# Score products in 64-column pairs, a separate place for each engine's part of a step, and a new order, in a fused attention and MLP kernel

## The chip, the cores and the metric

One core of one Trainium2 chip runs the whole program. The metric is the device time of one execution in microseconds (us). Engines are named as in the profile: PE (matrix products; PEld is its weight loads), DVE, ACT and POOL (elementwise work), SP (which issues nearly all transfers).

## What is computed

A linear attention with a decaying state, for 4 batches x 8 heads, 768 steps, head size 40, and behind it a gated MLP with a spatial gate over the sequence:

```python
for t in range(S):                       # attention, per batch and head
    y[t] = r[t] @ state
    Sa = state @ a[t]
    state = state * w[t][None, :] - outer(Sa, b[t]) + outer(v[t], k[t])
x = y as (4, 768, 320)                   # the heads side by side
h = gelu(x @ w_in)                       # 1024 columns
u, v = h[:, :512], h[:, 512:]
v = layernorm(v) * g_ln
v = w_sg @ v + b_sg                      # 768 x 768, over the sequence
out = x + (u * v) @ w_out
```

## The kernel before, in words

**Attention.** The 768 steps are cut into 12 chunks of 64 (`C`). Within a chunk the recurrence becomes matrix products and the inverse of a unit triangular 64x64 matrix for each of the 32 (batch, head). A chunk goes through these stages:

- *Gates*, once per batch: `gate_w` (L259) to `gate_k` (L314). DVE scans the decays (`ex`, `hs`), DVE or POOL multiplies them into `at` and `kb`, PE forms the products `ab` and turned copies of `kb` (`gate_4`, L289), DVE masks `ab` into `at` (`gate_a`), ACT copies the block to be inverted into `nts` (`gate_n`) and the turned `kb` into `kbt` (`gate_k`).
- *Inverse*, once per chunk for all 32: DVE turns the 32x32 blocks (`inv_in`, L319, tile `n`). Then `steps` (L328) does elimination steps, each a product `tg` and a sum `x`; for the chunks 2 to 11 POOL does them all but the last one, which is DVE's with the tile `tv`. In chunk 0 DVE and POOL share them, in chunk 1 DVE does the first step. `inv_back` (L373), `inv_g` (L385) and `inv_x` (L397) turn the result back and join the four 32x32 blocks with PE products (`gp`, `xp`) and ACT copies into `xt`.
- *Chain*, once per batch: `chain1` (L426) forms `ru`, `chain_t` (L436) turns the state (`tp`), `chain2` (L444) applies the inverse, `chain3` (L455) forms the next state (`sp`, first the old state through a 128-column identity product, then 8 pairs of products for the heads) and turns `vu` (`ut`), `chain4` (L481) forms the scores (`pq`, four products with 128 weight columns and 128 columns of data) and masks them on DVE (`pqs`), `chain5` (L490) forms the outputs (`yp`), which DVE scales (`yt`) and SP writes to the DRAM buffer `xd`.

Products in fp32 run on PE in several passes: the profile counts two for one matmul of the code, so 8 for the four score products of a batch.

**MLP.** The class `Mlp` reads `xd` back (`load_x`) and splits it into a high and a low fp32r half (`split_x`: `xh`, `xl`). Its pieces are `v0` to `v5` (`in_v`, PE tile `hv`, 8 products of 512 columns), `u0` to `u7` (`in_u`, `hu`), `s0` to `s7` (`sgu`, `sg`, 18 products of 384 columns) and `o0` to `o5` (`outp`, `op`, 10 to 12 products of 384 columns). A `v` piece ends in a normalised and split pair `vh`, `vl`, an `s` piece in a gated and split pair `gy`, `gx` (DVE twice, ACT, POOL). The weights of the gate are split into `wsh` on ACT and `wsl` on POOL or DVE (`part_sg`, string `SGE`); the output weights come as 64-bit numbers and go through `split64` (L710: ACT, DVE twice, ACT, POOL three times; tiles `sc`, `stg`, `lt`, `woh`, `wol`).

**Order.** Every engine executes its instructions in program order (class `InOrder`), so order is written out by hand. A chunk has 28 positions, a half of a chunk 14. `half` (L510) gathers the steps with their positions and sorts them: `CH` places the twelve chain steps of each half (a step is placed as a whole, with its PE, ACT and DVE parts), `GPOS` the gates, `START`, `BACK` and `GX` the inverse, `DEC` and `DSTEP` the conversion of the input weights, `FILL` and `AFTER` five MLP pieces and their elementwise parts within the last chunk. The first chunk's prologue (L567 to L588) has positions of its own: `T0` to `T4`, `TB0`, `TB1`, `ZERO`, `SECOND`, `EX`, and a letter per batch that says whether DVE (`V`) or POOL (`G`) does a gate product (`E0A`, `E0K` for chunk 0, `E1A`, `E1K` for chunk 1). Behind the chunks `Mlp.run` (L980) goes through the list `SEQ0` for batch 0 (mixed with the `v` and `u` pieces of batch 1) and `SEQ` for the others; `SGS`, `OUTS` and `OSTEP` say before which piece the weight conversions stand, and `XL` how many pieces ahead x is loaded.

Of the kernel before, what the change touches and what calls it, by code (L numbers as in the profile page):

```python
# [17 lines left out]
C = 64  # L18
# [3 lines left out]
DF = 1024  # L22
# [14 lines left out]
T0 = 6.16  # L37
T1 = 16.87
T2 = 5.22
TB0 = 4.1  # L40
TB1 = 11.89
# [3 lines left out]
T3 = 10.0  # L45
T4 = 16.8
CH = ((1.45, 2, 4, 5.28, 4.96, 7.81, 8.16, 12.33, 4.53, 10.76, 13.17, 14.9), (-1.88, 1.21, 7.06, 5.51, 8.13, 7.67,
    10.0, 10.99, 3.41, 8, 12, 14.21))
GPOS = (((0.34, 0.33, 0.61, 1.31, 3.87, 4.25, 4.26, 4.27), (2.52, 2.51, 2.79, 3.49, 5.81, 6.43, 6.44, 6.45), (5.06,
# [4 lines left out]
GE = ("VVVVV", "VVV", "V", "V")  # L54
START = (13.13, 0.58)
E0A = "GGGG"
E0K = "GVGG"
E1A = "GGGG"
E1K = "GVGG"
BACK = (17.88, 23.11, 26.9, 23.92)  # L60
GX = (24.68, 4.6)
# [4 lines left out]
DSTEP = ((-12.34, -2.5, 0.0, 0.98, 2.18, 3.84), (-13.26, -0.81, 0.0, 0.49, 2.66, 3.52))  # L66
DEC = ((275.05, 0), (277.2, 0), (283.29, 0), (288.37, 0), (292.22, 1), (298.29, 1), (299.11, 1), (306.81, 0),
    (311.6, 1), (314.23, 1), (324.86, 1), (328.18, 1))
# [3 lines left out]
FILL = (("x0", 0, 321.35), ("v0", 0, 329.24), ("v1", 0, 345.97), ("v2", 0, 347.7), ("u0", 0, 349.9))  # L72
AFTER = {"v": (0.56, 0.57, 1.47, 1.61, 1.95, 2.3, 2.4, 4.11, 4.8), "u": (0.5, 1.09, 1.99, 2.04), "x": ()}
# [5 lines left out]
SEQ0 = (("x1", 0), ("x0", 0), ("v0", 0), ("u3", 0), ("u0", 0), ("u1", 0), ("v2", 0), ("u2", 0), ("v1", 0), ("v3",  # L79
# [14 lines left out]
IS = 1  # L94
ROWS = (12, 26)
EX = ((0.01, 0, 0.3, 0.6, 1.5, 2.6, 2.61, 2.62), (0.01, 0, 0.3, 0.6, 1.5, 2.6, 2.61, 2.62))
# [47 lines left out]
def attention(tc, a, xd, flag, keep, ps, mlp=None):  # L144
# [4 lines left out]
    with ExitStack() as ctx:  # L149
# [73 lines left out]
        for i, t in enumerate(nts):  # L223
            for h in range(2):
                (V, G, G)[i].memset(t[64 * h + 32:64 * h + 64, :, 32:64], 0.0)
# [30 lines left out]

        gate, unit, x1_of, st2, pqt = {}, {}, {}, {}, {}
# [10 lines left out]
        def gate_2(c, b, E=V):  # L268
# [5 lines left out]
            E.tensor_tensor(out=at[:, :, 1], in0=kab[:, 1], in1=ex[:, :, 0:C], op=ALU.mult)  # L274
            A.copy(out=at[64:128, :, 0], in_=at[0:64, :, 1])

# [12 lines left out]
        def gate_4(c, b):  # L289
            kb, at = gate.pop((c, b)), ats[ent(c, b)]  # L290
            ab = gate[c, b] = ps("ab0"), ps("ab1")
            for p in range(NP):
                for h in range(2):
                    r = slice(64 * h, 64 * h + 64)
                    for x in range(2):
                        T.matmul(ab[h][64 * x:64 * x + 64, C * p:C * p + C], lhsT=kb[r, p, x], rhs=at[r, p, 1],
                                 start=True, stop=True, tile_position=(64 * h, 64 * x), skip_group_check=True)
# [3 lines left out]
        def gate_a(c, b):  # L301
            ab, at = gate[c, b], ats[ent(c, b)]
            for h in range(2):
                V.tensor_tensor(out=at[0:64, :, h], in0=ab[h][0:64, 0:256].rearrange("p (q x) -> p q x", x=C),
                                in1=mask[0:64].unsqueeze(1).broadcast_to([64, NP, C]), op=ALU.mult)

        def gate_n(c, b):
            nt, q0 = nts[c % 3], 4 * b
            for h in range(2):
# [4 lines left out]
        def gate_k(c, b):  # L314
            for g in range(2):
                A.copy(out=kbts[ent(c, b)][:, 160 * g:160 * g + 160].rearrange("p (q h x) -> p q h x", q=2, h=2),
                       in_=gate[c, b][g][:, 256:512].rearrange("p (q h x) -> p q h x", q=2, h=2)[:, :, :, 0:D])

        def inv_in(c):  # L319

            n = iv.tile([128, 32, 32], F32, name="n", bufs=2)
# [62 lines left out]

        def inv_g(c):  # L385
            nt, gs, x1z = nts[c % 3], gss[0], x1_of[c]
            gp = ps("gp")
            for q in range(NQ):
                for h in range(2):
                    r = 64 * h  # L390
                    T.matmul(gp[r + 32:r + 64, 32 * q:32 * q + 32], lhsT=nt[r:r + 64, q, 32:64],
                             rhs=x1z[r:r + 64, q], start=True, stop=True, tile_position=(r, r + 32))
            gv = gp.rearrange("p (q x) -> p q x", x=32)
# [3 lines left out]
        def inv_x(c):  # L397
# [7 lines left out]
            xv = xp.rearrange("p (q x) -> p q x", x=32)  # L405
            A.copy(out=xt[0:32, :, 32:64], in_=xv[0:32])
            A.copy(out=xt[64:96, :, 32:64], in_=xv[64:96])

        rus = {}
# [15 lines left out]

# [703 lines left out]
```

## Time and profile before

| | us |
|---|---|
| median of 3 runs (650.85 to 651.57) | 651.53 |
| the profiled execution | 653.22 |
| its span in the trace | 650.8 |

| engine | busy us | share of the span | instructions |
|---|---|---|---|
| PE | 584.3 | 90% | 9038 |
| PEld | 527.0 | 81% | 9038 |
| DVE | 509.4 | 78% | 1079 |
| ACT | 393.7 | 60% | 1106 |
| POOL | 394.5 | 61% | 881 |

The rows of the trace count from the start of the span. A timeline row gives start, duration of the whole group, engine, line, operation, output tile, inputs, shapes and the number of instructions in the group; in brackets stands how long the engine had been idle before it, and what ended that. All instructions have the line L130, since a helper records them, so tiles are told by their names. The granted clock of PE is given as a share of its full rate; 0.50 is the lower of its two levels.

### The profile page before, as it was taken

What the parts mean: (1) busy time and instruction counts of PE and PEld (TensorE: products, weight loads), DVE (VectorE), ACT (ScalarE), POOL (GpSimd) and SP (SyncE); (2) the same over time, 40 slices, a digit from 0 to 9 for tenths busy, and PEclk for the clock granted to TensorE, in tenths of its full rate; (3) what the DMA queues carried; (4) which work ended last, traced back from release to release, by engine and by line L of the source; (5) the groups of instructions that cost most, each with busy time, mean ns of one, the idle gap of its engine ahead of it and who ended that gap; (6) DMA issues with size and microseconds to landing.
All of it is one profiled execution on the core that took longest, in us unless ns stands there. A gap on an engine that the chain in (4) does not pass through costs nothing.

```text
span 650.8 us, 22488 instructions
## 1 busy us (share of the span) xinstructions
PE 584.3 (90%) x9038; PEld 527.0 (81%) x9038; DVE 509.4 (78%) x1079; ACT 393.7 (60%) x1106; POOL 394.5 (61%) x881
## 2 busy tenths in 40 slices
PE   6435899999999999999897999696999999999996
PEld 5334788888888888888786888596989999999995
DVE  7898977979779788797586789877888768567732
ACT  5535888888988879798573756442345336324410
POOL 6367888888888888888887344566442433332321
PEclk8556899999999999999977799798999999999999
DMA  7731333444444443334433316310003003010001
GB/s 238 213 101 42 106 105 106 118 108 119 112 112 117 117 120 108 103 98 104 117 101 85 109 40 181 120 56 17 31 1 104 26 7 103 1 32 13 20 29 38
DMA packets 57618, 56.55 MB, mean 87 GB/s; under 512 B 35936, under 2 KB 47456, under 8 KB 57504
## 3 DMA queue, kind: packets, MB, share of 16 engines
q1 hardware_dynamic: 57504, 55.02, 29.5%
q8 instruction: 73, 1.20, 0.8%
q14 instruction: 41, 0.34, 0.2%
HBM read 47.14 MB, written 7.86 MB: 85 GB/s over the span
## 4 chain that ended last, share of the span: by engine, by line
PE 40%; DVE 21%; POOL 20%; issue 8%; ACT 7%; DMA 2%; SPq 0%; POOLq 0%; ACTq 0%; DVEq 0%
PE sg L130 11%; POOL x L130 9%; POOL tg L130 9%; PE op L130 5%; PE ab L130 4%; PE hu L130 4%; PE hv L130 3%; PE sp L130 3%; PE pq L130 2%; PE yp L130 2%; PE ru L130 2%; DVE sc L130 2%; DVE v L130 2%; DVE x L130 2%; DVE g L130 2%
## 5 line engine op out<-in xcount | busy, mean ns | idle before, releaser
L130 POOL TENSOR_TENSOR x<-x,tg 128x100 f32<-128x100 f32 (+8 forms) x348 | 131.8, 379 | 27.0
L130 POOL TENSOR_TENSOR tg<-x,n 128x100 f32<-128x100 f32 (+8 forms) x348 | 125.4, 360 | 29.3 <-DVE x L130 2.2
L130 POOL TENSOR_TENSOR gx<-g,gy 128x384 fp32r<-128x384 f32 x32 | 33.2, 1041 | 79.7 <-ACT gy L130 79.7
L130 PE MATMUL sg<-wsh,vh 128*128 128x384 f32 x192 | 67.1, 350 | 4.3 <-ACT vh L130 3.6
L130 PE MATMUL sg<-wsl,vh 128*128 128x384 f32 x192 | 66.6, 347 | 3.7 <-POOL wsl L130 3.0
L130 ACT ACTIVATE nts<-ab 32x256 f32<-32x256 f32 x192 | 62.2, 324 | 10.6 <-DVE at L130 7.8
L130 PE MATMUL sg<-wsh,vl 128*128 128x384 f32 x192 | 66.7, 347 | 0.8 <-POOL vl L130 0.8
L130 PE MATMUL ab<-at,kb 64*64 64x64 f32 x1536 | 42.2, 241 | 22.2 <-POOL kb L130 13.6
L130 ACT CAST gy<-g 128x384 fp32r<-128x384 f32 x32 | 16.5, 515 | 70.7 <-DVE g L130 66.9
L130 PEld LDWEIGHTS ab<-at,kb 64*64 64x64 f32 x1536 | 33.9, 148 | 30.9 <-POOL kb L130 15.6
L130 PE MATMUL pq<-rt,vut 128*128 128x128 f32 x384 | 56.3, 291 | 0.3 <-DVE yt L130 0.3
L130 PEld LDWEIGHTS pq<-rt,vut 128*128 128x128 f32 x384 | 48.2, 197 | 2.8 <-DVE yt L130 0.4
L130 PE MATMUL yp<-pqs,kbt 128*64 128x64 f32 x768 | 49.6, 235 | 0.0
L130 PE MATMUL yp<-rt,s 80*40 80x64 f32 x704 | 46.0, 231 | 0.0
L130 ACT CAST vh<-v 128x512 fp32r<-128x512 f32 x24 | 14.9, 622 | 50.2 <-DVE v L130 50.2
L130 POOL TENSOR_TENSOR rs<-rs,mhalf 128x1 f32<-128x1 f32 x24 | 13.5, 562 | 49.7 <-DVE rs L130 43.9
L130 POOL TENSOR_TENSOR vl<-v,vh 128x512 fp32r<-128x512 f32 x24 | 31.7, 1322 | 18.4 <-ACT vh L130 18.3
L130 PEld LDWEIGHTS yp<-pqs,kbt 128*64 128x64 f32 x768 | 40.1, 147 | 2.7 <-issue 1.1
L130 PEld LDWEIGHTS sg<-wsh,vh 128*128 128x128 f32 x192 | 37.4, 195 | 5.1 <-ACT vh L130 4.0
L130 PEld LDWEIGHTS sg<-wsl,vh 128*128 128x128 f32 x192 | 37.6, 196 | 4.6 <-POOL wsl L130 3.4
L130 DVE SCALAR_TENSOR_TENSOR g<-sg,gl,bt 128x384 f32<-128x384 f32 x32 | 19.7, 615 | 25.5 <-PE sg L130 24.4
L130 DVE TENSOR_TENSOR at<-ab,mask 64x256 f32<-64x256 f32 x96 | 35.8, 408 | 3.9 <-PE ab L130 3.2
(139 smaller groups left out, 1681.1 us busy)
## 6 DMA issues: line engine op xcount, KB each, us to landing
main<-main SPq DMA_DIRECT2D x88, 160.8 KB
vu<-vs SPq DMA_DIRECT2D x24, 160.0 KB
vs<-vb SPq DMA_DIRECT2D x24, 160.0 KB
rt<-rt SPq DMA_DIRECT2D x48, 80.0 KB
vut<-vt SPq DMA_DIRECT2D x24, 160.0 KB
xd<-yt SPq DMA_DIRECT2D x96, 40.0 KB
xt<-xd SPq DMA_DIRECT2D x16, 192.0 KB
out<-y SPq DMA_DIRECT2D x16, 192.0 KB
```

What stands on the lines that cost most here:

```text
L130: return self.tc.keep_in_program_order(f(*a, **k))
```

## The change

Scores: each of the four products of a batch becomes two with 64 weight columns, which write the two halves of the same output (`PQ`). State: the identity product is split into two of 64 columns and the head products load 40 weight columns instead of 64 (`MK`). `gate_4` runs its two inner loops in the other order. `gate_c`, the ACT copy of `gate_2`, gets a position of its own, and so does each engine's part of `inv_g`, `inv_x` and the chain steps (`LAG`, `GL`); a part whose position falls behind the end of a half goes into the next one (`tail`). Two gate products of the prologue go from POOL to DVE (`E0A`, `E1A`). In the last chunk six products that nothing reads, of 128 weight columns and 512 columns of data, stand at position 348.88 (`JUNK`). In the MLP the piece `v1` of batch 1 goes from before `s5` to behind `s4`, the last batch gets an order of its own (`SEQL`: `s6` and `s7` before `o0`), its last pairs `gy` and `gx` use tiles of `v` pairs that are free by then, and the weight conversions shift. All positions are set anew. `NS` is 0, so its branches aren't taken; they are left out below, as are assertions on the order.

```diff
-T0 = 6.16
-T1 = 16.87
-T2 = 5.22
+T0 = 7.03
+T1 = 16.19
+T2 = 3.25
...
-E0A = "GGGG"
+E0A = "VGGG"
-E1A = "GGGG"
+E1A = "GGVG"
...
-FILL = (("x0", 0, 321.35), ("v0", 0, 329.24), ("v1", 0, 345.97), ("v2", 0, 347.7), ("u0", 0, 349.9))
+FILL = (("x0", 0, 318.12), ("v0", 0, 332.67), ("v1", 0, 345.97), ("v2", 0, 345.98), ("u0", 0, 349.9))
...
-    0), ("s0", 0), ("s3", 0), ("v1", 1), ("v0", 1), ("s5", 0), ("s4", 0), ("o1", 0), ("u0", 1), ("o0", 0), ("v2",
-    1), ("o2", 0), ("s6", 0), ("s7", 0), ("v5", 1), ("u1", 1), ("v3", 1), ("v4", 1), ("u4", 1), ("o5", 0), ("o3",
+    0), ("s0", 0), ("s3", 0), ("v0", 1), ("s5", 0), ("s4", 0), ("v1", 1), ("o1", 0), ("u0", 1), ("o0", 0), ("v2",
+    1), ("o2", 0), ("s6", 0), ("s7", 0), ("u1", 1), ("v3", 1), ("v4", 1), ("v5", 1), ("u4", 1), ("o5", 0), ("o3",
...
-XL = 3
+XL = 2
-SGS = (2, 5, 5, 6, 8, 10, 10, 13, 12, 13, 14, 13)
-OUTS = (11, 12, 12, 14, 15, 16, 17, 18)
-OSTEP = (-2, 0, 0, 0, 0, 1)
-SGE = "GGGGGVGGGVGG"
+SGS = (2, 5, 3, 6, 8, 10, 10, 13, 14, 13, 14, 13)
+OUTS = (11, 12, 12, 14, 15, 18, 19, 18)
+OSTEP = (-2, 0, 0, 0, 0, 0)
+SGE = "GGGGGVGVGVGG"
...
-SECOND = (18.63, 0.02)
-ZERO = 3.22
+SECOND = (18.03, 0.07)
+ZERO = 3.51
...
+PQ = 1
+MK = 40
+JUNK = ((348.88, 6),)
...
+SEQL = ("s1", "s2", "s0", "s3", "s4", "s5", "s6", "s7", "o0", "o1", "o2", "o3", "o5", "o4")
...
         def gate_4(c, b):
...
-                for h in range(2):
-                    r = slice(64 * h, 64 * h + 64)
-                    for x in range(2):
+                for x in range(2):
+                    for h in range(2):
...
         def chain3(c, b):
...
-                    T.matmul(sp[:, 0:NP * D], lhsT=ident, rhs=sc.rearrange("p q x -> p (q x)"), start=True, stop=True,
+                for h in range(2 if IS else 0):
+                    r = slice(64 * h, 64 * h + 64)
+                    T.matmul(sp[r, 0:NP * D], lhsT=ident[:, r], rhs=sc.rearrange("p q x -> p (q x)"), start=True, stop=True,
                              skip_group_check=True)
                 for p in range(NP):
                     for h in range(2):
                         l0 = 2 * D * p + D * h
-                        T.matmul(sp[64 * h:64 * h + 64, D * p:D * p + D], lhsT=kbt[:, l0:l0 + 64],
+                        T.matmul(sp[64 * h:64 * h + m, D * p:D * p + D], lhsT=kbt[:, l0:l0 + m],
...
         def chain4(c, b):
...
-            for g in range(4):
-                T.matmul(pq[:, 128 * g:128 * g + 128], lhsT=vut[:, g], rhs=rt[:, :, g], start=True, stop=True)
+                for g in range(4):
+                    for x in range(2 if PQ else 0):
+                        T.matmul(pq[64 * x:64 * x + 64, 128 * g:128 * g + 128], lhsT=vut[:, g, x], rhs=rt[:, :, g], start=True,
+                                 stop=True, skip_group_check=True)
...
         def half(c, hf, side):
...
+            def put(k, fs):
+                d = lag[k] if len(fs) > 2 else (lag[k],)
+                for y, f in zip((0, *d), fs):
+                    add(z[k] + y, f)
...
+    def idle(self, n):
+        o = self.ps("idle")
+        for _ in range(n):
+            self.T.matmul(o, lhsT=self.wih[:, 0, HF:HF + 128], rhs=self.wih[:, 0, HF:DF], start=True, stop=True,
+                          skip_group_check=True)
```

## Rows read from the trace of the kernel before

**Rows 1.** Windows view: PE, PEld, DVE, ACT, POOL busy (instructions), clock, DMA share, GB/s.

```profile
75.00:351.00 276.00, 266.53 (x6403) 234.42 (x6402) 223.88 (x480) 225.58 (x691) 228.27 (x610) 0.98 0.40 110
```

**Rows 2.** Groups of POOL from 75 to 350 us: count, busy, mean ns, idle before.

```profile
L130 POOL TENSOR_TENSOR x<-x,tg 128x78 f32<-128x78 f32 (+4 forms) x303 | 116.6, 385 | 23.7
L130 POOL TENSOR_TENSOR tg<-x,n 128x78 f32<-128x78 f32 (+4 forms) x304 | 111.0, 365 | 23.8
```

**Rows 3.** Timeline of DVE and POOL in the prologue, and the last inversion step.

```profile
17.99 0.91 DVE L130 TENSOR_TENSOR at<-ab,mask 64x256 f32<-64x256 f32 x2 [1.38 <-PE ab L130]
31.15 1.28 DVE L130 TENSOR_TENSOR x<-x,tv 128x115 f32<-128x115 f32 x1
49.87 2.08 DVE L130 STREAM_TRANSPOSE n<-nts 128x1024 f32<-128x1024 f32 x1
...
52.44 0.24 POOL L130 TENSOR_TENSOR tg<-x,n 128x30 f32<-128x30 f32 x1 [2.22 <-DVE x L130]
...
350.81 0.25 POOL L130 TENSOR_TENSOR x<-x,tg 128x30 f32<-128x30 f32 x1
```

**Rows 4.** Groups by shape: one product of the gates on DVE.

```profile
L130 DVE TENSOR_TENSOR at<-main,ex 128x256 f32<-128x256 f32 x40 | 21.6, 540 | 0.0
```

**Rows 5.** Timeline of PE, narrow windows: scores, outputs, next chunk's sums, state.

```profile
255.50 0.61 PE L130 MATMUL pq<-rt,vut 128*128 128x128 f32 x4
...
255.83 0.28 PE L130 MATMUL pq<-rt,vut 128*128 128x128 f32 x1
256.04 0.29 PE L130 MATMUL ab<-at,kb 64*64 64x64 f32 x4
...
257.52 0.67 PE L130 MATMUL sp<-vu,kbt 128*64 128x40 f32 x16
...
260.25 0.28 PE L130 MATMUL yp<-rt,s 80*40 80x64 f32 x4
260.36 0.32 PE L130 MATMUL ru<-vs,at 128*64 128x40 f32 x6
```

**Rows 6.** Timeline: chunk 3's matrices turned on DVE, first used by POOL.

```profile
99.25 2.20 DVE L130 STREAM_TRANSPOSE n<-nts 128x1024 f32<-128x1024 f32 x1
...
105.75 0.24 POOL L130 TENSOR_TENSOR tg<-x,n 128x31 f32<-128x31 f32 x1
```

**Rows 7.** Timeline of PE: 18 products of the sixth `sgu` piece.

```profile
436.58 0.34 PE L130 MATMUL sg<-wsh,vh 128*128 128x384 f32 x1
...
438.67 0.34 PE L130 MATMUL sg<-wsh,vh 128*128 128x384 f32 x1
442.05 0.44 PE L130 MATMUL sg<-wsl,vh 128*128 128x384 f32 x1 [3.04 <-POOL wsl L130]
...
443.07 0.52 PE L130 MATMUL sg<-wsh,vh 128*128 128x384 f32 x1
...
446.27 0.41 PE L130 MATMUL sg<-wsl,vh 128*128 128x384 f32 x1
```

**Rows 8.** Timeline of POOL before that wait, of DVE after it.

```profile
440.19 0.80 POOL L130 TENSOR_TENSOR wol<-stg,lt 128x256 fp32r<-128x256 f32 x1
440.95 1.04 POOL L130 TENSOR_TENSOR wsl<-ws,wsh 128x384 fp32r<-128x384 f32 x1
...
449.98 0.60 DVE L130 SCALAR_TENSOR_TENSOR g<-sg,gl,bt 128x384 f32<-128x384 f32 x1
```

**Rows 9.** Waits of PE from 400 to 460 us: total, times, longest.

```profile
PE hv L130 <- DVE xh L130: 1.5, 1, 1.5
PE op L130 <- ACT gy L130: 1.2, 1, 1.2
PE op L130 <- POOL gx L130: 0.9, 2, 0.5
```

**Rows 10.** Waits of PE from 640 us to the end.

```profile
PE op L130 <- POOL gx L130: 0.5, 1, 0.5
PE op L130 <- ACT gy L130: 0.4, 1, 0.4
```

More of the change, by code (lines that the diff above doesn't have):

```diff
@@ L317, in gate_k @@
                        in_=gate[c, b][g][:, 256:512].rearrange("p (q h x) -> p q h x", q=2, h=2)[:, :, :, 0:D])
+            seen.add(("kt", c, b))
         def inv_in(c):
+            for h in range(2 if NS else 0):
+                r = slice(64 * h + 32, 64 * h + 64)
+                A.copy(out=nts[c % 3][r, :, 0:32], in_=nts[c % 3][r, :, 32:64])
             n = iv.tile([128, 32, 32], F32, name="n", bufs=2)
@@ L427, in chain1, with mm @@
             at, vs, rb = ats[ent(c, b)], vss[b // 2][:, b % 2], rhsb[b]
-            ru = rus[b] = ps("ru")
             k = 128 if c else 64
-            for p in range(NP):
-                for h in range(2):
-                    T.matmul(ru[64 * h:64 * h + 64, D * p:D * p + D], lhsT=at[0:k, p, h],
-                             rhs=vs[0:k, p, h], start=True, stop=True, skip_group_check=True)
-            A.copy(out=rb, in_=ru[:, 0:NP * D].rearrange("p (q x) -> p q x", x=D))
+            def mm():
+                assert not c or ("vs", c, b) in seen
+                assert ("at", c, b) in seen
+                ru = rus[b] = ps("ru")
+                for p in range(NP):
+                    for h in range(2):
+                        T.matmul(ru[64 * h:64 * h + 64, D * p:D * p + D], lhsT=at[0:k, p, h],
+                                 rhs=vs[0:k, p, h], start=True, stop=True, skip_group_check=True)
+                seen.add(("c1", c, b))
@@ L436, in chain_t, with out, mm @@
+            def out():
+                A.copy(out=rb, in_=rus[b][:, 0:NP * D].rearrange("p (q x) -> p q x", x=D))
+                seen.add(("rb", c, b))
+            return mm, out
         def chain_t(c, b):
-            if c:
-                tp = ps("tp")
+            def mm():
+                tp = tps[b] = ps("tp")
                 for g in range(2):
                     T.transpose(out=tp[0:80, 128 * g:128 * g + 128], in_=scs[b][:, 2 * g:2 * g + 2], identity=ident)
+                seen.add(("ct", c, b))
@@ new lines, in mm, with out @@
+            def mm():
+                assert ("rb", c, b) in seen and ("xt", c) in seen
+                ru = rus[b]
+                for p in range(NP):
+                    for h in range(2):
+                        r = slice(64 * h, 64 * h + 64)
+                        T.matmul(ru[r, 160 + D * p:160 + D * p + D], lhsT=xt[r, 4 * b + p], rhs=rb[r, p],
+                                 start=True, stop=True, tile_position=(64 * h, 64 * h), skip_group_check=True)
+            def out():
+                uv = rus[b][:, 160:320].rearrange("p (i g x) -> p i g x", i=2, g=2)
+                for h in range(2):
+                    A.mul(out=vu[64:128, :, h], in_=uv[64 * h:64 * h + 64], mul=-1.0)
+                seen.add(("vu", c, b))
@@ L472, in chain3, with copies @@
                 V.tensor_tensor(out=sc[0:e], in0=ts, in1=bc(cn[0:e], [e, NP, D]), op=ALU.mult)
+                seen.add(("sc", c, b))
+            def copies():
+                if c == NCH - 1:
+                    return
+                assert ("c1", c, b) in seen and ("sc", c, b) in seen
                 for h in range(2):
@@ L481, in chain4, with out @@
+            def out():
+                assert ("tn", c, b) in seen and (not c or ("c4", c - 1, b) in seen)
+                A.copy(out=vuts[b // 2][0:80, b % 2, :, 1], in_=uts[b][0:80, 0:256].rearrange("p (q t) -> p q t", q=4))
+                seen.add(("ut", c, b))
+            return mm, state, copies, turn, out
         def chain4(c, b):
             rt, vut = rts[b // 2][:, b % 2], vuts[b // 2][:, b % 2]
-            pq = ps("pq")
-            for g in range(4):
-                T.matmul(pq[:, 128 * g:128 * g + 128], lhsT=vut[:, g], rhs=rt[:, :, g], start=True, stop=True)
@@ new lines, in mm @@
+            def mm():
+                assert ("ut", c, b) in seen
+                pq = pqt[b] = ps("pq")
+                for g in range(4):
+                    for x in range(2 if PQ else 0):
+                        T.matmul(pq[64 * x:64 * x + 64, 128 * g:128 * g + 128], lhsT=vut[:, g, x], rhs=rt[:, :, g], start=True,
+                                 stop=True, skip_group_check=True)
+                    if not PQ:
+                        T.matmul(pq[:, 128 * g:128 * g + 128], lhsT=vut[:, g], rhs=rt[:, :, g], start=True, stop=True)
+                seen.add(("c4", c, b))
@@ L510, in half, with loads @@
+        def loads(f, stage, c, bs, *a):
+            assert all((stage, c, b) in seen for b in bs)
+            f(*a)
         def half(c, hf, side):
@@ L953, in side @@
                 at(PX1, lambda: self.load_x(1, 0))
+            for p, k in JUNK:
+                at(p, lambda k=k: self.idle(k))
             for x, b, p in FILL:
@@ L974, in piece @@
             self.sgu(b, k % 4, k // 4)
+        elif x[0] == "j":
+            self.idle(k)
         elif x[0] == "o":
```

219 lines of the change are left out of this document (140 added, 79 removed), and 9 rows, old and new, of the table GPOS.

## The prediction, made before the changed kernel was run

> **What bounds the kernel now.** I read the share of each engine by stretches first. From 75 to 351 us PE is busy for 266.5 of 276 us at a clock of 0.98, and POOL for 228 [rows 1]: two engines that look near their limit, so the groups of instructions have to say which one sets the pace. On POOL the elimination sums and products take 116.6 and 111.0 us, with 23.7 and 23.8 us of idle time before them, and no releaser is named for that idle time [rows 2]. Together that is 275.1 of 275 us: POOL goes from one step to the next, and the gaps of some 80 ns are its own. In this stretch POOL sets the pace, chunk after chunk, and PE is only almost as long. The third view is the timeline around it. POOL's first step of the long series starts at 52.44 and its last sum stands at 350.81 [rows 3], so the time has three parts: a prologue of 52.4 us, a POOL chain of 298.6 us (with the last sum's 0.25), and a tail of 299.7 us to the end of the span at 650.8.
>
> The prologue hangs on DVE, which runs from its first scan to the block that it turns at 49.87 with small holes only; POOL waited 2.22 us for it [rows 3]. The tail is read from the waits of PE, which has the most work there.
>
> The sum below is made against the profiled execution, 653.2 us, which lies 1.7 us above the median of 651.5; the last step takes 1.7 off.
>
> **The change part by part.**
>
> *Scores.* The last four of a batch's eight score passes start from 255.50 on, the very last at 255.83, and the next kind at 256.04 [rows 5]. So a pass takes 0.11 us, and the last one 0.21: some 0.10 is the price of going over to another shape of tile. The change makes 16 passes of 64 columns of weights. Output products in such a shape go four in 0.11 us (260.25 to 260.36), that is two at a time at the pace of one full pass, and from there to the sums of the next chunk no 0.10 is seen [rows 5]. Two halves side by side thus cost what one full product does, and spare up to two changes of shape, some 0.1 to 0.2 us a batch. Against this stands a rule. The Trainium skill, in "TensorE: Matmul & The Clock Gate", section "Part 3: Packing small matmuls", says that a weight load overlaps with running products only when it goes to another group of rows. Both halves use all 128 rows, so by that rule they would run in turn, and the scores would double. The pace of the outputs in rows 5, which have the same form, speaks against it; it is a rival below.
>
> *State.* Eight pairs take from 257.52 on 0.67 us of a group, loads of 64 columns [rows 5]. Loading 40 columns can at best save three eighths of what the load sets, some 0.1 to 0.2 us a batch, and at worst nothing; the identity in two halves is priced like the scores, at nothing. Scores and state together save some 0.3 us a batch, 1.2 a chunk, on PE.
>
> *What of it counts in the middle.* Nothing, as long as POOL goes on without a gap [rows 2]. PE's savings there only lengthen its lead. If POOL's cover were gone, ten chunks by 1.2 us plus the order would be worth about 16 us at most, but no edit here touches POOL's steps. The new positions can do harm only if an input of POOL comes late: the blocks of chunk 3 are turned from 99.25 to 101.45 and first used at 105.75 [rows 6], a lead of 4.3 us. I take 0, with a bound of nothing below and, for a late block, the rival below. The same holds for the separate places of ACT's and DVE's parts, the other loop order in `gate_4` and the ACT copy `gate_c`: ACT is busy for 226 and DVE for 224 of the 276 us [rows 1], and both end ahead of POOL.
>
> *Prologue.* Chunk 1's gates start two positions earlier, zeros are loaded later, and two products go from POOL to DVE. On DVE they add 2 x 0.54 = 1.1 us [rows 4]. In return DVE's hole of 1.38 us before the masking at 17.99 [rows 3], with a smaller one ahead of it 1.7 us in all, has a filling: the masking waited for PE, PE for POOL's products. And sums such as the one at 31.15 took 1.28 us; a smaller one of the kind took 0.25 on POOL at 350.81 [rows 3]. There are two of these, both while POOL works on gate products; with POOL relieved they should shrink by 1.0 each. That gives -1.7 + 1.1 - 2.0 = -2.6. Bounds: +1.1 if neither hole nor contention goes, -4 if smaller contended operations shrink too.
>
> *Last chunk.* Six score groups of a batch lie between 351 and 400 us, where PE has no POOL chain beside it: -1.2 with the state products. The six idle products are 512 columns; products of 384 go at 0.174 us (12 from 436.58 to 438.67 [rows 7]), so one is 0.232 by columns and six 1.4 us. They stand between other work, not in a wait that I can name, so I count +1.3 to +1.4; the lower bound is 0 if PE would have waited there. Together +0.1. PE's wait for `xh`, 1.5 us [rows 9], lies behind DVE's queue; I leave it, and take its going as an end of the range.
>
> *Weights and gates of the MLP.* PE stood 3.04 us before the product at 442.05, for POOL's `wsl` [rows 7]. POOL did that one at 440.95, right behind the low part of an output weight that ended there [rows 8], and nothing needed that weight yet. The change brings these low parts forward by a piece, and gives one `wsl` to DVE: POOL is 1.3 us shorter and the queue ahead of the one that PE waits for is gone. Behind the wait PE went at 0.32 us a product instead of 0.174 (10 from 443.07 to 446.27 [rows 7]), the lower clock after 3 us without work: 1.5 us more, which goes with the wait. Then the first `op` waited 1.2 us for `gy` and 0.9 for `gx` [rows 9]: DVE had reached the `s3` gate only at 449.98 [rows 8], in line behind conversions of output weights. Two of those go two pieces later, so these 2.1 us go as well. Together -3.0 - 1.5 - 2.1 = -6.6. What is late next is the `s` piece's next weight, or `v1`'s pair, now made three pieces later; what DVE takes on (1.3 us) it must find between 440 and 460 us. So the gain can be anything down to 0, if each wait only moves.
>
> *End.* In the last batch `s6` and `s7` now come before `o0` to `o2`, whose 32 products of 0.174 us = 5.6 us cover their splits; PE's last waits, 0.5 and 0.4 us [rows 10], go: -0.9.
>
> **Sum.** 653.2 - 2.6 + 0 + 0.1 - 6.6 - 0.9 = 643.2 for an execution like the profiled one, 641.5 beside the median. Its own range is 637 to 647: prologue between -4 and +1, a third of the waits left, or the `xh` wait gone too.
>
> **The rivals.**
>
> *Less.* The waits at 442 and 450 only move: prologue and end remain, -2.6 + 0.1 - 0.9 = -3.4, so 648. For it speaks that DVE gets more work just there; against it, that the waits have a named cause in the queue, which is taken out.
>
> *More.* The transition clears wholly: the wait for `xh` goes (1.5), the second stretch of lower clock behind the `op` waits too (1.6 by the same difference of pace), the first `s` piece finds its weights in time (1 to 3), and the prologue gives 4: 8 us more, some 633.
>
> *Slower: score halves in turn.* If two halves don't run side by side, a batch's 16 passes take 16 x 0.11 = 1.8 us instead of 0.9, so PE has 3.6 us a chunk more, less 0.6 for the state. PE's 266.5 of 276 us leave 0.9 a chunk, so from about 0.4 us a batch on PE takes the pace over from POOL. Then ten chunks at some 2 us give +20, less what the tail gains: about 662. A second place on this side is the turned block, if it comes more than 4.3 us later; each us beyond that costs ten.
>
> *No effect.* The new order only does what the old one did, and the idle products eat the rest: 651.5.
>
> **How the numbers follow.** The forecast has 0.55, less 0.20, more 0.11, slower 0.09, no effect 0.05. The range goes from 632 to 650: it holds the first three cases, and leaves out slower, no effect and the tail of more. About 0.2%, 1.3 us, is what a measurement of this kernel can tell from no change. Faster by more than that: 0.86; within it: 0.05; slower: 0.09.
>
> **What the changed profile would show.** POOL's `tg` and `x` with the same sums and no releaser, the first step at 50 us instead of 52.4 and the last sum 298 us behind it. Score groups on PE that go over into the next kind without the extra 0.10. PE from 436 to 460 us with no wait of a us and no stretch at half clock, and no wait behind 640. I am wrong if the POOL chain itself gets longer or shorter (the middle was not POOL's alone), if a score batch on PE takes over 1.3 us, or if the time from POOL's last sum to the end stays at 300.

## The result and the profile after

The changed kernel takes 643.44 us (median of 4 runs, 642.61 to 643.88) where the kernel before takes 651.19 us beside it: a ratio of 0.988, 95% interval 0.9863 to 0.9897, 7.75 us faster. The forecast was 641.5 us with a range of 632 to 650.

The profiled execution took 643.88 us, the slowest of the four. From its page, the span, the busy times of the engines, and the group of the score products:

```profile
span 642.2 us, 23467 instructions
...
PE 566.1 (88%) x9516; PEld 507.3 (79%) x9516; DVE 499.7 (78%) x1082; ACT 388.3 (60%) x1106; POOL 393.0 (61%) x878
...
L140 PE MATMUL pq<-rt,vut 128*64 128x128 f32 x768 | 54.8, 288 | 4.6 <-ACT kbt L140 4.0
```

PE has 478 more instructions than before, and is busy for 18 us less (566.1 instead of 584.3). The score passes are 768 instead of 384.

The three parts of the time, read where the prediction read them [rows 3]. The timeline of POOL, the first step of the long series and its last sum:

```profile
50.98 0.24 POOL L140 TENSOR_TENSOR tg<-x,n 128x30 f32<-128x30 f32 x1 [5.60 <-DVE x L140]
...
348.73 0.25 POOL L140 TENSOR_TENSOR x<-x,tg 128x30 f32<-128x30 f32 x1
```

The series starts at 50.98 instead of 52.44 and ends at 348.98 instead of 351.06, so it takes 298.0 us instead of 298.6. From there it is 293.2 us to the end instead of 299.7. The tail can be cut further at the first `s` piece (from 410.28 to 408.02 us) and the seventh (from 461.73 to 455.61), both read from PE's timeline:

| part | predicted | in the profiled executions |
|---|---|---|
| prologue, to POOL's first step | -2.6 | -1.5 |
| POOL's series | 0 | -0.6 |
| last chunk, to the first `s` piece | +0.1 | -0.2 |
| weights and gates, to the seventh `s` piece | -6.6 | -3.9 |
| from there to the end | -0.9 | -2.5 |
| span | -10.0 | -8.6 |

(The executions themselves differ by 9.3 us and the medians by 7.75, because the profiled execution before, 653.22 us, lay 2.0 us above the median of 651.19, and the one after 0.4 above its own.)

**The middle.** One row of the windows, columns as in [rows 1], and four of PE's timeline, for a batch's scores, the next product, and the state:

```profile
75.00:350.00 275.00, 254.03 (x6758) 219.42 (x6754) 223.03 (x480) 219.51 (x688) 227.52 (x609) 0.97 0.39 107
```

```profile
349.08 1.09 PE L140 MATMUL pq<-rt,vut 128*64 128x128 f32 x16
350.11 0.41 PE L140 MATMUL tp<-ident,sc 128*80 128x128 f32 x2
350.45 0.49 PE L140 MATMUL sp<-sc,ident 128*64 128x160 f32 x4
350.77 0.47 PE L140 MATMUL sp<-vu,kbt 128*40 128x40 f32 x16
```

POOL's group of elimination products from 75 to 345 us: count, busy, mean ns, idle before, with no releaser named, as in [rows 2]:

```profile
L140 POOL TENSOR_TENSOR tg<-x,n 128x56 f32<-128x56 f32 (+5 forms) x298 | 109.1, 366 | 23.3
```

POOL is busy for 227.5 of 275 us, as before. PE is busy for 254.0 of 275 where it was for 266.5 of 276. The 16 score passes take from 349.08 to 350.11, 1.03 us, about what the 8 passes took with the change to the next kind [rows 5]. The last of them starts at 349.90, so the step to the next kind is still 0.21 us; the forecast had its extra 0.10 go. The state takes 0.73 us from 350.45 to 351.18.

**The prologue.** DVE's waits from 5 to 50 us, first the one of the kernel before that the change was to fill, then two of the changed kernel:

```profile
DVE at L130 <- PE ab L130: 1.7, 2, 1.4
```

```profile
DVE ex L140 <- DMA main<-main: 0.6, 1, 0.6
DVE x L140 <- ACT x L140: 0.5, 1, 0.5
```

Two groups of DVE's timeline in the changed kernel, then POOL's product beside the first of them, and the one that stood beside DVE's sum at 31.15 in the kernel before:

```profile
31.03 1.45 DVE L140 SCALAR_TENSOR_TENSOR x<-n,x 128x26 f32<-128x26 f32 x3
...
34.01 0.28 DVE L140 TENSOR_TENSOR x<-x,tv 128x115 f32<-128x115 f32 x1
```

```profile
31.25 1.19 POOL L140 TENSOR_TENSOR kb<-main,hs 128x512 f32<-128x512 f32 x1 [2.19 <-DVE x L140]
```

```profile
31.12 1.18 POOL L130 TENSOR_TENSOR kb<-main,hs 128x512 f32<-128x512 f32 x1 [2.53 <-DVE tv L130]
```

The wait of 1.7 us for `ab` is gone, and the sum of 128x115 that took 1.28 us [rows 3] takes 0.28. But two waits are new, 0.6 us for `main` and 0.5 for `x`, and three row steps at 31.03 now take 1.45 us together, where three of about this shape took 0.55 us before (at 26.62). One of the three runs from 31.33 to 32.48, beside POOL's `kb` from 31.25 to 32.44. In the kernel before the slow sums at 31.15 and 36.86 (1.28 and 1.25 us) ended 0.13 us behind a `kb` of POOL each.

**Behind the chunks.** PE's waits from 400 to 460 us, the rows that answer to [rows 7, 9]:

```profile
PE sg L140 <- ACT vh L140: 3.6, 1, 3.6
PE op L140 <- ACT gy L140: 1.8, 1, 1.8
PE sg L140 <- POOL wsl L140: 1.4, 1, 1.4
PE op L140 <- POOL gx L140: 0.8, 1, 0.8
```

The wait for `wsl` fell from 3.0 to 1.4 us, `gx` from 0.9 to 0.8, and `gy` rose from 1.2 to 1.8. Of the two stretches at half clock behind 440 us in the kernel before (0.50 from 444 to 446 us and from 454 to 456), the first is gone with the shorter wait. One remains, behind the wait for `gy` (0.50 from 446 to 448 us). The stretch at half clock behind the wait of 3.6 us for `vh` stands in both kernels.

### The profile page after: what moved, and what is told of

Same layout as the page of the kernel before. It is cut to its first block, busy times and chain, and to the rows that moved or that the text cites. A ratio compares the mean times of both kernels' runs of the same rounds, so it can differ in the third digit from the quotient of the medians.

```text
span 642.2 us, 23467 instructions
## 1 busy us (share of the span) xinstructions
PE 566.1 (88%) x9516; PEld 507.3 (79%) x9516; DVE 499.7 (78%) x1082; ACT 388.3 (60%) x1106; POOL 393.0 (61%) x878
## 4 chain that ended last, share of the span: by engine, by line
PE 44%; DVE 19%; POOL 16%; ACT 10%; issue 7%; DMA 3%; SPq 0%; POOLq 0%; DVEq 0%; ACTq 0%
PE sg L140 13%; POOL x L140 7%; PE op L140 7%; POOL tg L140 7%; PE hv L140 5%; PE hu L140 5%; PE pq L140 3%; ACT nts L140 3%; DVE at L140 2%; PE ru L140 2%; PE ab L140 2%; DVE ex L140 2%; DVE x L140 2%; DMA main<-main 2%; PE yp L140 2%
## 5 line engine op out<-in xcount | busy, mean ns | idle before, releaser
L140 POOL TENSOR_TENSOR gx<-g,gy 128x384 fp32r<-128x384 f32 x30 | 31.7, 1061 | 63.2 <-ACT gy L140 59.4
L140 PE MATMUL pq<-rt,vut 128*64 128x128 f32 x768 | 54.8, 288 | 4.6 <-ACT kbt L140 4.0
L140 PE MATMUL ab<-at,kb 64*64 64x64 f32 x1536 | 39.5, 240 | 15.8 <-POOL kb L140 7.8
L140 PEld LDWEIGHTS pq<-rt,vut 128*64 128x64 f32 x768 | 43.1, 142 | 11.4 <-ACT kbt L140 7.1
L140 PEld LDWEIGHTS ab<-at,kb 64*64 64x64 f32 x1536 | 32.1, 148 | 22.9 <-POOL kb L140 8.9
L140 PE MATMUL yp<-pqs,kbt 128*64 128x64 f32 x768 | 46.3, 226 | 0.3 <-ACT vut L140 0.2
L140 PE MATMUL yp<-rt,s 80*40 80x64 f32 x704 | 42.8, 221 | 0.8 <-issue 0.8
L140 DVE TENSOR_TENSOR pqs<-pq,mask 128x512 f32<-128x512 f32 x48 | 31.9, 682 | 14.0 <-PE pq L140 14.0
L140 PEld LDWEIGHTS yp<-pqs,kbt 128*64 128x64 f32 x768 | 38.4, 138 | 3.7 <-ACT vut L140 1.3
L140 PE MATMUL ru<-rhsb,xt 64*64 64x40 f32 x768 | 30.1, 235 | 11.4 <-ACT xt L140 7.4
```

Of the source, the lines that this page charges most:

```text
L140: return self.tc.keep_in_program_order(f(*a, **k))
```

## The experiments

All are made from the changed kernel. Their ratios are to the kernel before, so they stand against 0.988 (0.9863 to 0.9897); one thousandth is 0.65 us.

### Scores as one product

```diff
-PQ = 1
+PQ = 0
```

> The changed kernel with the scores put back to one product of 128 weight columns each; all else as changed. Theory (POOL sets the pace of the middle, the score halves are worth little): the POOL series from its first to its last step stays at 298 us within 0.5, the time is that of the changed kernel (0.988 of before) within 1 us. Rival (the changed order lives on PE time that the halves free): the series grows by several us and the ratio comes to 0.995 or more.

641.91 us, ratio 0.9864 (0.9826 to 0.9902). POOL's series runs from 50.30 to 347.56, 297.3 us. The theory holds in its main point: the series does not grow, and neither does the time (both lie a little below the ranges named, 298 us within 0.5 and 643.4 within 1). The halves are worth nothing that can be measured here. Counting from each start of PE to its next one, between 100 and 315 us (eight chunks), the halves take 33.1 us and the whole products 33.6.

### No idle products

```diff
-JUNK = ((348.88, 6),)
+JUNK = ()
```

> The changed kernel without the six idle products. Theory (they stand between other work and only cost): PE is 1.4 us shorter in the last chunk and the time falls by 1.0 to 1.4 us, to 641.7 to 642.4. Rival one (they keep PE's clock up): behind their place a stretch at 0.50 appears and the time rises by 1 us or more. Rival two (PE waits there or right behind anyway, for x or for the first pair of v): the time stays within 0.5 us.

644.26 us, ratio 0.9882 (0.9848 to 0.9915): leaving 1.45 us of work out (386.73 to 388.18 in the changed kernel) gains nothing that shows, though an interval of 2 us to each side would still hold the gain of 1.0 to 1.4 us that the theory named. The traces say more. The start of a `v` piece in PE's timeline without them, then the same in the changed kernel:

```profile
395.19 0.50 PE L140 MATMUL hv<-wih,xh 128*128 128x512 f32 x1 [1.72 <-DVE xh L140]
...
397.10 1.48 PE L140 MATMUL hv<-wih,xh 128*128 128x512 f32 x3
398.38 1.41 PE L140 MATMUL hv<-wil,xh 128*128 128x512 f32 x3
```

```profile
397.33 0.50 PE L140 MATMUL hv<-wih,xh 128*128 128x512 f32 x1 [0.88 <-DVE xh L140]
...
398.82 0.84 PE L140 MATMUL hv<-wih,xh 128*128 128x512 f32 x3
399.50 0.84 PE L140 MATMUL hv<-wil,xh 128*128 128x512 f32 x3
```

Without the idle products PE gets to the next `v` piece earlier, and waits 1.72 us for `xh` instead of 0.88. A good microsecond after that wait three products of 512 columns take 1.28 us instead of 0.68: half clock (0.66 is the mean from 395 to 400 us, against 1.00). From the last `yp` product to the first `s` piece it is 20.9 us instead of 18.0. In all twelve other profiles with the idle products that stretch takes 18.0 us. Of the 2.9 us more, 0.8 are the longer wait and some 2 the slower pace: in the trace the idle products bring more than the 1.45 us that they cost. Rivals one and two each hold in part; the theory, which priced the idle products at +1.4 us, is not borne out.

### Order and weight conversions of the MLP as before

```diff
-SGS = (2, 5, 3, 6, 8, 10, 10, 13, 14, 13, 14, 13)
-OUTS = (11, 12, 12, 14, 15, 18, 19, 18)
-OSTEP = (-2, 0, 0, 0, 0, 0)
-SGE = "GGGGGVGVGVGG"
+SGS = (2, 5, 5, 6, 8, 10, 10, 13, 12, 13, 14, 13)
+OUTS = (11, 12, 12, 14, 15, 16, 17, 18)
+OSTEP = (-2, 0, 0, 0, 0, 1)
+SGE = "GGGGGVGGGVGG"
...
```

(`SEQ0` and `XL` too.)

> The changed kernel with the list of pieces of batch 0 and the places of the weight conversions (SEQ0, XL, SGS, OUTS, OSTEP, SGE) as before. Theory (the waits around 440 us are set by these lists): 3.9 us of the gain go, the product for wsl waits some 3 us again and a stretch at half clock follows; 647.3, ratio 0.994. Rival (the waits only follow from how early the pieces come, or were shortened by the earlier end of the chunks): the time stays within 1 us of 643.4.

648.27 us, ratio 0.9949 (0.9929 to 0.9969): 4.5 us of the gain are gone, as the theory had it. PE's waits from 400 to 460 us:

```profile
PE sg L140 <- POOL wsl L140: 3.7, 1, 3.7
```

The wait for `wsl` is back, and half clock follows it (0.50 from 440 to 442 us). This is the largest part of the change, 4.5 of 7.75 us. Six settings go back at once here, so which of them holds the gain is not shown.

### The last batch in the old order

```diff
-            seq += [(x, b + (x[0] in "uvx")) for x in (SEQL if b == B - 1 else SEQ)] if b else list(SEQ0)
+            seq += [(x, b + (x[0] in "uvx")) for x in SEQ] if b else list(SEQ0)
```

> The changed kernel with the order of the last batch as in the other batches (s6 and s7 behind o0 to o2). Theory: PE's waits for the last gates come back, the end is 0.9 to 1.5 us longer, 644.3 to 644.9. Rival (the tiles taken from free pairs shorten the end, not the order): within 0.4 us of 643.4.

643.13 us, ratio 0.9869 (0.9838 to 0.99): by the times undecided. PE's waits from 455 us to the end, of which the changed kernel has none:

```profile
PE op L140 <- POOL vl L140: 0.5, 1, 0.5
PE op L140 <- ACT vh L140: 0.4, 1, 0.4
```

These are the 0.5 and 0.4 us of [rows 10] again, under other tile names, since the last pairs now lie in the `v` tiles; these tiles alone, which the rival named, don't take the waits away. From the product `fp` (a small one behind the chunks, at 530.95 us in the changed kernel, with the same pieces behind it in every kernel up to the last batch) to the end of the span it is 112.6 us, against 111.2 in the changed kernel, 112.8 before. So the end is 1.4 us longer in the trace, and the time that the theory forecast (644.3 to 644.9) did not come; in the times that is lost in the scatter of what comes earlier (below).

### The prologue as before

```diff
-T0 = 7.03
-T1 = 16.19
-T2 = 3.25
+T0 = 6.16
+T1 = 16.87
+T2 = 5.22
...
-E0A = "VGGG"
+E0A = "GGGG"
...
-E1A = "GGVG"
+E1A = "GGGG"
...
```

> The changed kernel with the eleven constants of the prologue (T0 to T4, TB0, TB1, SECOND, ZERO, E0A, E1A) as before. Theory (the earlier first step is theirs): POOL's series starts at 52.4 instead of 51.0 us and the time grows by 1.5 us, ratio 0.990. Rival (the other loop order of the gate products or the ACT copy in its own place brought it): it still starts at 51.0 within 0.4.

643.4 us, ratio 0.9898 (0.9879 to 0.9917), about 1.2 us over the ratio of the changed kernel, with intervals that overlap. POOL's first step of the series:

```profile
52.10 0.24 POOL L140 TENSOR_TENSOR tg<-x,n 128x30 f32<-128x30 f32 x1 [2.12 <-DVE x L140]
```

52.1 us, against 49.96 to 51.68 in the other profiles taken by then of kernels with the new prologue (mean 50.8 of eight). DVE's wait for `ab` is back too, with 2.0 us. Some 1.3 us of the earlier first step are in these constants; in the times the part is within the noise.

### More work for PE, and the old products

The scores twice (first), half of them twice (second):

```diff
-                for g in range(4):
+                for g in [k for k in range(4) for _ in range(2)]:
                     for x in range(2 if PQ else 0):
```

```diff
-                for g in range(4):
+                for g in (0, 0, 1, 2, 2, 3):
                     for x in range(2 if PQ else 0):
```

The products as before, in the new order:

```diff
-PQ = 1
-MK = 40
+PQ = 0
+MK = 64
...
-                for h in range(2 if IS else 0):
-                    r = slice(64 * h, 64 * h + 64)
-                    T.matmul(sp[r, 0:NP * D], lhsT=ident[:, r], rhs=sc.rearrange("p q x -> p (q x)"), start=True, stop=True,
+                if IS:
+                    T.matmul(sp[:, 0:NP * D], lhsT=ident, rhs=sc.rearrange("p q x -> p (q x)"), start=True, stop=True,
```

> The changed kernel with every score product done twice over into the same output: 4.1 us more of PE work a chunk (33.06 us in eight chunks). Theory (POOL sets the pace, PE has 26.9 - 26.1 = 0.8 us a chunk to spare): a chunk then takes PE 30.2 us, POOL's series grows by 10 x 3.3 = 33 us, time some 675, and POOL's groups show waits. Rival one (PE's spare is the 21 of 275 us that the share of busy time shows, 2.0 us a chunk): +20, some 663. Rival two (score passes lie in PE's waits): under +5.

> The changed kernel with half of the score products done twice: 2.1 us more of PE work a chunk. Theory (0.8 us a chunk to spare): +10 x 1.3 = 13 us, some 656. Rival one (2.0 us to spare): within 2 us of 643.4. Both ask whether the pace goes over from POOL to PE between the two.

> The changed kernel with scores, identity product and state loads as before; only order and lists are changed. PE gets 1.2 us a chunk back (9.6 us in eight chunks). Theory (hidden behind POOL in the middle): POOL's series stays at 298 us within 1, time 643.4 to 644.4. Rival (PE has only 0.8 us a chunk to spare, so 0.4 of the 1.2 comes through): series +4 us, time 647 to 648.

POOL's group of elimination products from 75 to 345 us in each: count, busy, mean ns, idle before and its releasers. The old products, half of the scores twice, all twice:

```profile
L140 POOL TENSOR_TENSOR tg<-x,n 128x45 f32<-128x45 f32 (+5 forms) x298 | 109.5, 367 | 24.3 <-DVE n L140 1.1
```

```profile
L140 POOL TENSOR_TENSOR tg<-x,n 128x56 f32<-128x56 f32 (+5 forms) x294 | 107.2, 365 | 28.5 <-DVE n L140 5.8
```

```profile
L140 POOL TENSOR_TENSOR tg<-x,n 128x70 f32<-128x70 f32 (+5 forms) x287 | 103.5, 361 | 36.1 <-DVE n L140 13.7 <-ACT rhsb L140 0.6
```

| kernel | PE work a chunk | wait of POOL for `n` | series | time | ratio |
|---|---|---|---|---|---|
| as changed | 25.6 | 0 | 298.0 | 643.44 | 0.9880 (0.9863 to 0.9897) |
| old products | +1.2 | 1.1 | 298.4 | 645.17 | 0.9918 (0.9887 to 0.9949) |
| half of the scores twice | +1.8 | 5.8 | 302.3 | 647.54 | 0.9953 (0.9937 to 0.9969) |
| all twice | +3.5 | 13.7 | 310.4 | 662.04 | 1.0192 (1.0164 to 1.0219) |

The 25.6 us are PE's busy time from 100 to 315 us (204.55 us) over eight chunks. The added work is measured: a score group takes 1.10 us on average as changed, 1.54 with half of it twice and 1.98 with all of it, four groups a chunk; the expectations took 2.1 and 4.1, since they doubled the step to the next kind too.

The pace goes over from POOL to PE between the first and the third row. Half twice gave +4.1 us, between theory (13) and rival one (2). All twice gave +18.6, near rival one (+20): of it 12.4 in the series and 5.4 between its end and the first `s` piece, where PE works without POOL. With the old products the first wait of POOL for `n` shows, and the time is 1.7 us longer by the medians, 2.5 by the ratios, with intervals that just overlap; it lies between the times that theory and rival named, while the series stays where the theory had it. So the cheaper products leave the series alone only just: they are the slack that keeps the turned blocks in time.

The traces show the bound itself. In the kernel before, the changed one and the nine variants that keep the cheaper state products and repeat no scores, POOL's series has 51.5 us of idle time each, and no gap over 0.15 us. Their series still differ, from 296.7 to 298.6 us, by POOL's own steps. With the old products there are two longer gaps, 1.1 us together, with half of the scores twice six (5.8 us), with all twice nine (14.3 us).

Of the 9.7 us that the products of eight chunks save on PE, 5.9 are the state's pairs (19.4 to 13.5 us, loads of 40 columns instead of 64), 3.1 the identity in halves (13.4 to 10.3), and 0.7 the scores (33.7 to 33.1), all counted from start to start between 100 and 315 us. No run takes back the other loop order of `gate_4` or the place of `gate_c`.

### Ways to a faster kernel

**Weights later.** ACT's timeline of the changed kernel behind POOL's last sum:

```profile
352.63 0.42 ACT L140 ACTIVATE lt<-lt 128x256 f32<-128x256 int32 x1 [3.52 <-DVE lt L140]
...
354.28 0.61 ACT L140 ACTIVATE vu<-ru 64x160 f32<-64x160 f32 x2
```

ACT stands 3.5 us for a conversion, and `vu`, which is ready, comes behind it.

```diff
-DEC = ((275.89, 0), (276.0, 0), (281.98, 0), (286.85, 0), (290.7, 1), (297.59, 1), (298.13, 1), (305.09, 0),
+DEC = ((275.89, 0), (276.0, 0), (281.98, 0), (286.85, 0), (290.7, 1), (303.5, 1), (304.0, 1), (305.09, 0),
```

> The changed kernel with two conversions of input weights (the sixth and seventh of DEC) moved from positions 297.6 and 298.1 behind the join of chunk 11's blocks, to 303.5 and 304.0. Theory (behind POOL's last sum the way to the last outputs runs through the queues of ACT and DVE: ACT stands 3.5 us before lt with the copy of vu behind it, PE then waits 2.2 us for vu): vu comes by 350 instead of 354 us, the stretch from POOL's last sum to the last output product falls from 38.6 to 41 us in the traces so far to 36 or 37, and 1.5 to 3 us of it reach the end: 640.5 to 642. Rival (the weights are wanted soon after, or x1 sets the place of the first gate): the stretch is shorter, PE waits as much longer for xh, time within 1 us of 643.4.

648.21 us, ratio 0.9952 (0.9936 to 0.9968): 4.7 us slower. Three groups of ACT, and one of PE:

```profile
346.63 1.25 ACT L140 ACTIVATE vu<-ru 64x160 f32<-64x160 f32 x4 [0.57 <-PE ru L140]
...
352.86 1.11 ACT L140 ACTIVATE sc<-stg 128x256 f32<-128x256 f32 x3 [3.76 <-DMA stg<-w_in]
...
364.36 0.43 ACT L140 ACTIVATE sc<-stg 128x256 f32<-128x256 f32 x1 [3.24 <-DMA stg<-w]
...
366.97 0.43 PE L140 MATMUL ru<-rhsb,xt 64*64 64x40 f32 x2 [5.58 <-ACT xt L140]
```

`vu` does come at 346.6, as forecast. But the later conversions give back their staging tiles later, so the next weights are loaded later, and ACT stands 3.8 and 3.2 us for these transfers, with the copies of chunk 11's inverse behind it: PE waits 5.6 us for `xt`. The stretch to the last outputs is 46.4 us instead of 41. Neither theory nor rival had that.

**x of batch 1.** DVE's timeline of the changed kernel ahead of the first `s` piece's wait of 3.6 us for `vh`:

```profile
407.42 2.84 DVE L140 TENSOR_TENSOR xl<-xt,xh 128x384 fp32r<-128x384 f32 x2 [0.82 <-ACT xh L140]
410.29 0.56 DVE L140 TENSOR_TENSOR xh<-xt,xh 64x384 fp32r<-64x384 f32 x1
...
412.67 0.53 DVE L140 TENSOR_SCALAR v<-v,mv,rs 128x512 f32<-128x512 f32 x1
```

3.4 us of x splits, and 0.8 us of waiting for them, stand ahead of the `v` pieces that the first `s` piece needs; the next `v` is normalised at 412.67. Three ways to change that: the split behind the first `s` piece, its low halves on POOL, and the split just ahead of that piece:

```diff
-    0), ("v4", 0), ("v5", 0), ("x0", 1), ("u4", 0), ("u6", 0), ("u5", 0), ("u7", 0), ("s1", 0), ("x1", 1), ("s2",
+    0), ("v4", 0), ("v5", 0), ("u4", 0), ("u6", 0), ("u5", 0), ("u7", 0), ("s1", 0), ("x0", 1), ("x1", 1), ("s2",
```

> The changed kernel with the split of batch 1's first x half moved from behind v5 to behind the first s piece. Theory (the first s piece waits 3.6 us for vh because DVE does 4 us of x splits ahead of the last two v pieces): that wait falls under 1 us, the lower clock behind it goes, and 2 to 4 us reach the end: 639.5 to 641.5. Rival (DVE is what bounds the whole stretch from 410 to 445 us): the wait moves behind the gates s1 to s3 or to v0 of batch 1, time within 1 us of 643.4.

```diff
-            self.split(h[:, k, c], l[:, k, c], t[:, k], self.A, self.V)
+            self.split(h[:, k, c], l[:, k, c], t[:, k], self.A, self.G if b == 1 else self.V)
```

> The changed kernel with the low halves of batch 1's x (four subtractions of 384 columns) on POOL instead of DVE. Theory (DVE bounds the stretch from 410 to 445 us, POOL is idle for some 8 us between 411 and 424): DVE is relieved by 4 to 5 us, the waits for vh and for gy fall together by 2 us or more, time 640 to 641.5. Rival (POOL's vl and wsl then come later, or the two engines slow each other): within 1 us of 643.4 or slower.

```diff
-    0), ("v4", 0), ("v5", 0), ("x0", 1), ("u4", 0), ("u6", 0), ("u5", 0), ("u7", 0), ("s1", 0), ("x1", 1), ("s2",
+    0), ("v4", 0), ("v5", 0), ("u4", 0), ("u6", 0), ("u5", 0), ("u7", 0), ("x0", 1), ("s1", 0), ("x1", 1), ("s2",
```

> The changed kernel with the split of batch 1's first x half behind u7, one piece ahead of the first s piece, instead of behind that piece as in the run before. Theory (the wait for vh stays away, and the split is ahead of the output weights in the queues of ACT and DVE, so the 1.9 us wait for xh at the first v of batch 1 goes too): 638.5 to 640, ratio 0.981. Rival (DVE bounds the stretch as a whole, the wait only shows elsewhere): 640 to 641.5 like the run before.

| kernel | time | ratio |
|---|---|---|
| x split behind the first `s` piece | 640.67 | 0.9835 (0.9816 to 0.9853) |
| low halves on POOL | 640.86 | 0.9835 (0.9812 to 0.9858) |
| x split ahead of the first `s` piece | 642.89 | 0.9874 (0.9851 to 0.9897) |

The first two beat both kernels, by 2.9 us against the changed one by the ratios, with intervals that don't meet its own, and both as their theories had it. PE's waits from 400 to 460 us in the three, in this order:

```profile
PE sg L140 <- ACT wsh L140: 2.1, 2, 1.5
PE sg L140 <- POOL wsl L140: 1.9, 1, 1.9
PE hv L140 <- DVE xh L140: 1.9, 1, 1.9
PE op L140 <- ACT gy L140: 1.1, 1, 1.1
```

```profile
PE sg L140 <- POOL wsl L140: 3.1, 1, 3.1
PE sg L140 <- ACT vh L140: 2.5, 1, 2.5
```

```profile
PE sg L140 <- ACT wsh L140: 4.6, 4, 1.5
PE sg L140 <- POOL wsl L140: 3.1, 2, 1.9
```

In the first the wait for `vh` is gone, and what is late next is weights (2.1 and 1.9 us) and the split itself (1.9 for `xh`); half clock, which the theory had go, is there still (0.50 from 412 to 418 us). In the second `vh` is shorter (2.5) and `gy` gone, and `wsl` on POOL is late (3.1). In the third the wait for `xh` is gone as forecast, but PE waits 4.6 and 3.1 us for weights instead: the wait shows elsewhere, as the rival had it, and the time, 642.89 us, lies above both forecasts. The profiled executions of the first and the third end at 638.9 and 639.2 us, closer than their medians. A combination of the first two was not run.

## Why the prediction was right, and where it was not

**The bound of the middle** was named rightly: POOL's series, untouched, sets the pace, and PE's savings (1.2 us a chunk, predicted and measured) don't show in it. That their sum came out is luck in part. Of a batch's 0.3 us, 0.1 to 0.2 were put down to changes of shape around the scores, which stay: the scores save 0.02 us. The identity in halves was priced at nothing and saves 0.10; the head products save 0.19, in their range. PE's room was off too. The prediction gave the kernel before 0.9 us a chunk, from the share of busy time; from 100 to 315 us PE is idle there for 3.1 us in eight chunks, 0.4 a chunk, and in the changed kernel for 10.4, 1.3 a chunk. Putting the old products back (+1.2 a chunk) brings the first wait of POOL, so the savings were closer to deciding than "nothing as long as POOL goes on" makes it sound: they were needed as room.

**The rival of score halves in turn** (662 us) fell: 16 passes take what 8 did. The rule of the Trainium skill, in "TensorE: Matmul & The Clock Gate", section "Part 3: Packing small matmuls", that weight loads overlap only for different groups of rows would, as the prediction read it, have doubled them; here the measurement decides against that. The rival's price was met all the same, by luck: with 3.5 us more of PE work a chunk, where it assumed 3.6, the time was 662.04. Its sum had the middle 20 us longer than before and all of the gains outside it kept. In the run POOL's series is 11.8 us longer than before (310.4 instead of 298.6), and behind it 1.7 us of the gain are left.

**The prologue** was forecast at -2.6 and gave -1.5 in the trace. The step that failed is the term for DVE's holes: the 1.7 us went, but 1.1 us of new ones opened, for `main` and for `x`. The two slow sums did shrink, from 1.28 and 1.25 to 0.28 and 0.32, but another group of row steps grew by 0.9, so that term was about twice what came. What went to DVE were two `at` products; the slow sums had stood beside POOL's `kb` products, and these stayed on POOL, so one of them now stands beside the row steps. The two products on DVE took 0.41 us each, 0.8 together instead of 1.1.

**The idle products** were priced at +1.4 us, as work between other work. The step that failed is that they only cost, with no wait beside them. Taking them out gained nothing: they fill part of a wait for `xh`, and in the trace without them that wait is longer (1.72 us instead of 0.88) and half clock follows.

**Weights and gates** were forecast at -6.6 and gave -3.9 in the trace, 4.5 in the times. The mechanism is shown: with the old lists the wait for `wsl` comes back. The size was off, since both waits were taken as gone. `wsl` still waits 1.4 us, and the first `op` waits 1.8 for `gy` and 0.8 for `gx`. These waits, and the half clock that is gone behind the first (1.5 us by the prediction's count), make up -2.6 of the -3.9; 0.8 more came in the first four `s` pieces (22.7 us before, 21.9 after), which the prediction had not counted. What holds `gy` up is DVE's queue. Three rows of the changed kernel, PE's two waits and DVE's gate of `s0`, for which the `op` waits:

```profile
434.82 0.44 PE L140 MATMUL sg<-wsl,vh 128*128 128x384 f32 x1 [1.41 <-POOL wsl L140]
...
444.01 0.44 PE L140 MATMUL op<-gy,woh 128*128 128x384 f32 x1 [1.79 <-ACT gy L140]
...
442.16 0.61 DVE L140 SCALAR_TENSOR_TENSOR g<-sg,gl,bt 128x384 f32<-128x384 f32 x1
```

PE had ended `s0` at 426.9, so DVE is some 15 us behind PE here: what its queue gains for one piece, another piece waits for. With the low halves of x on POOL the wait for `gy` was gone, which bears this out. The prediction named that as the rival "less", and the truth lies between it and the forecast.

**The end** was forecast at -0.9 and gave -1.6 from `fp` on, of which 1.4 go back with the old order; another 0.9 came between the seventh `s` piece and there, where PE's 0.4 us wait for `y` is gone, which the prediction had not counted.

The sum came near because the errors partly cancel, which is luck: weights and prologue gave 3.8 us less, the last chunk, the series and the end 2.5 us more. By the times only the 4.5 us of the MLP lists are clear of noise; about 1.2 for the prologue and some 2 for the products have intervals that overlap with the changed kernel's, and the end is inside the scatter. Of the signs that the prediction named, two failed: the score groups still have their 0.21 us before the next kind, and from 436 to 460 us, where PE should have had no wait of a us and no half clock, it has a wait of 1.8 us and a stretch at 0.50.

## What to carry to other kernels

Where one engine runs without a gap and a second is only almost as long, cheaper work on the second gains nothing by itself, but it is the room that a new order needs: add work to it and see at which size the first one starts to wait. Where an engine's instructions run long beside a certain product of another engine, look whether it is that product that the change moves; if it stays, the next instruction can run long beside it. Before a wait is booked as gain, look which queue it stands in; if that queue is late as a whole, moving work out of it (to an idle engine, or behind the next consumer) gains where new places within it only move the wait. A step that is put later also gives its buffers back later, and the next load starts from there.

## What the runs showed of the hardware

- Two products of 64 weight columns that share the 128 rows and write different halves of the output ran side by side: the passes of a pair start 6 or 7 ns apart, and 512 passes took 0.065 us each, against 0.131 for 256 whole ones.
- In the prologue DVE's instructions beside a `kb` of POOL (1.18 us) took about as long as it: 1.28 and 1.25 us before, 1.16 in the changed kernel, where the same kinds took 0.2 to 0.3 us elsewhere. What the two share is not shown.
- A wait of PE of 1.72 us was followed by 3 us at half clock about a microsecond later; one of 0.88 us at the same place was not, nor was one of 1.5 us there in the kernel before [rows 9]. Six useless products before it brought more in the trace than the 1.45 us that they cost, and by the times nothing that can be told from noise.
- Two executions with the same instructions up to there differ by 2.4 us between POOL's last sum and the last output (41.0 and 38.6 us). In one PE waits 1.88 us for `xt` and runs 30 products at half clock, in the other 0.42 us and full clock; in the second the half clock fell earlier, from 354 to 358 us, behind a wait of 2.2 us for `vu`. PE's timeline of the changed kernel, then of the one with the old order of the last batch:

```profile
363.71 0.31 PE L140 MATMUL ru<-rhsb,xt 64*64 64x40 f32 x2 [1.88 <-ACT xt L140]
364.31 1.92 PE L140 MATMUL ru<-rhsb,xt 64*64 64x40 f32 x30 [0.29 <-ACT xt L140]
```

```profile
362.87 0.31 PE L140 MATMUL ru<-rhsb,xt 64*64 64x40 f32 x2 [0.42 <-ACT xt L140]
363.47 1.12 PE L140 MATMUL ru<-rhsb,xt 64*64 64x40 f32 x30 [0.29 <-ACT xt L140]
```

This scatter is larger than several parts of the change, so those were read from the trace from a fixed point on, not from the total. What makes the clock fall at the one place or the other stays open.
